# A two-stage kernel's hand-written order table replaced by another, searched with a later landing for DMA transposes

## The chip, the cores and the metric

The kernel runs on one core of a Trainium2 chip. The metric is device time in microseconds (us) of one execution; the value for a kernel is the median of several executions. The core has a matrix engine (TensorE, PE in the profile), a vector engine (VectorE, DVE), a scalar engine (ScalarE, ACT), GpSimd (POOL) and a sync engine (SyncE, SP) that here only issues DMAs. Each engine runs its own instructions in the order in which the program gives them; between engines, semaphores make one wait for another.

## The reference

Two stages, the first an attention with a decaying state, the second a mixing layer. Shapes: 4 batches, 8 heads, 768 tokens, head width 48 (8 x 48 = 384 channels).

```
for t in range(S):
    kt, vt, rt = (k[:, :, t], v[:, :, t], r[:, :, t])
    cur = np.einsum('bhd,bhe->bhde', u[None] * kt, vt)
    y[:, :, t] = np.einsum('bhd,bhde->bhe', rt, state + cur)
    state = w[None, :, :, None] * state + np.einsum('bhd,bhe->bhde', kt, vt)
...
theta = x @ w_theta
cos_t, sin_t = (np.cos(theta), np.sin(theta))
zr = x * cos_t
zi = x * sin_t
yr = np.einsum('ts,bsd->btd', w_tok_r, zr)
yi = np.einsum('ts,bsd->btd', w_tok_i, zi)
y = yr + yi
u = x + y
return (u + np.maximum(u @ w_ch, 0.0)).astype(np.float32)
```

Here x is the attention's y with the heads side by side, 4 x 768 x 384.

## The kernel before

**Tiling.** A batch's 768 tokens are 6 chunks of 128; two chunks make a pair. There are 12 pairs, numbered 0 to 11 over the batches. `attention` (one call for each pair) loads r, k and v, multiplies r and k by powers of the decay (`rscale`, line 567; `kscale`, 580 or 583), turns both so that the channels lie along the partitions (the "R flip" and "K flip": matmuls against the identity, line 530, then a copy out of PSUM), makes scores (631) and masks them (637), adds the product of r and k for the diagonal (PD, line 644 in batch 0 and 650 later; its sums at 659 go through `dg` to `yd`, 666), updates the state (outer 690, S 708 and 718), and makes the outputs (730, 735), to which line 742 adds yd: that is x in bf16. In batch 0 two tokens share a partition in the loads, and v is spread by matmuls (615).

**The turn of x and u.** x is turned to xT for theta (760). The first six pairs do this on TensorE, with a copy out of PSUM; from pair 6 on, `turn` (line 543) does it with a DMA transpose, issued from SP. theta is followed by sine and cosine on ACT (764, 767), and by zr on DVE (770) and zi on GpSimd (773). `mixing` (one call for each pair) sums 12 matmuls for each chunk over the batch's six zr and six zi chunks (791, two matmuls in a task), adds x (`un`, 800), turns the result to uT (on TensorE in pairs 0 to 3 and 11, by DMA transpose in pairs 4 to 10), multiplies with w_ch (`f`, the channel matmul, 817), finishes on DVE (`fin`, 821) and stores (825). The token weights are cast (291 or 289) and turned on TensorE (514) as they arrive, and copied from PSUM.

**Fillers.** 108 tasks of two matmuls on zeros (834) need no data. They stand in TensorE's order where the table puts them, and 32 of them after the last channel matmul.

**What sets the order.** `build` only describes the work: each call of `P.add` is a task with the engines that may run it, each with a pair of planned costs in ns (time on the engine, and time from then until the result can be used), and with what it reads and writes. 925 tasks come out. The order is written out in `ORDER`: one entry for each task, with its number, its engine (0 PE, 1 DVE, 2 ACT, 3 POOL, 4 SP) and, where it takes PSUM banks, their numbers. `follow` walks the table and emits the tasks; the planned costs are not used then. They were used by a search outside the program that made the table. In it, `lock=SHARED` marks tasks of DVE and POOL that the planner does not let overlap; when the program runs, nothing keeps them apart, unless data does.

The lines that set the transposes' planned cost and the order:

```
def turn(dst, src, prio, rd, wr, name):
    P.add({SP: (1600, 1500)}, lambda e: nc.sync.dma_start_transpose(out=dst, in_=src),
          rd=rd, wr=wr, prio=prio - 2e6, name=name)
...
for seq, e, *tiles in table:
    t = self.tasks[seq]
    assert all(d.seq in done for d in t.deps)
    done.add(seq)
    t.eng = ENGINES[e]
```

All loads, stores and transposes go through SP's one queue in table order; an entry that waits for a buffer or for data holds those behind it.

Of the kernel before, what the change touches and what calls it, by code (L numbers as in the profile page):

```python
# [27 lines left out]
    (0, 2), (4, 1), (13, 3), (2, 1), (3, 1), (16, 0, 7), (1, 2), (146, 4), (14, 3), (17, 0, 5),  # L28
    (7, 2), (145, 4), (8, 3), (10, 3), (9, 1), (32, 0, 2), (5, 1), (33, 0), (18, 2), (34, 0),
    (144, 4), (20, 2), (35, 0), (153, 3), (36, 0), (37, 0), (23, 2), (38, 0), (39, 0), (15, 3),  # L30
    (24, 2), (40, 0), (41, 0), (22, 2), (154, 0, 6, 0), (12, 3), (186, 4), (150, 1), (19, 2), (42,
    0), (21, 2), (11, 1), (43, 0), (6, 1), (44, 0), (25, 0, 3), (187, 4), (45, 0), (46, 0), (151,
    0, 5), (26, 1), (30, 1), (27, 2), (147, 1), (47, 0), (167, 0, 4), (152, 2), (48, 0), (49, 0),
    (50, 0), (168, 1), (51, 0), (188, 4), (52, 0), (53, 0), (28, 2), (54, 0), (155, 2), (55, 0),
    (189, 1), (31, 3), (56, 0), (148, 0, 3), (156, 2), (169, 0), (149, 2), (190, 0, 0), (229, 4),
    (192, 1), (57, 0), (58, 0), (59, 0), (191, 2), (60, 0), (61, 0), (157, 0, 1, 7), (170, 1),
    (62, 0), (63, 0), (163, 1), (64, 0), (228, 4), (193, 0, 6), (158, 1), (65, 0), (66, 0), (67,
    0), (195, 2), (68, 0), (69, 0), (164, 0, 5), (159, 1), (70, 0), (71, 0), (160, 0, 3, 4), (165,
    2), (194, 2), (230, 4), (166, 3), (196, 0, 1, 0), (161, 1), (72, 0), (73, 0), (209, 0, 7),
    (198, 2), (162, 1), (197, 2), (171, 0, 6), (140, 4), (234, 1), (74, 0), (210, 2), (75, 0),  # L40
    (76, 0), (202, 0, 3, 1), (29, 2), (199, 0, 0, 4), (172, 1), (231, 3), (173, 0, 5), (280, 4),
    (201, 1), (77, 0), (211, 0), (203, 1), (235, 0, 6), (272, 4), (237, 2), (78, 0), (79, 0),
    (174, 1), (80, 0), (81, 0), (82, 0), (83, 0), (212, 1), (84, 0), (236, 2), (232, 0, 4), (142,
    4), (205, 1), (85, 0), (86, 0), (87, 0), (251, 0, 7), (268, 4), (233, 2), (204, 1), (281, 3),
    (175, 0, 6), (200, 1), (88, 0), (141, 2), (206, 0, 1), (276, 4), (89, 0), (90, 0), (247, 1),
    (91, 0), (238, 0, 3, 0), (207, 2), (252, 2), (176, 1), (208, 3), (241, 0, 5, 4), (292, 4),
    (248, 0, 1), (240, 2), (243, 1), (213, 0, 7), (143, 2), (92, 0), (215, 0, 6), (242, 1), (249,
    2), (273, 2), (244, 0, 0, 4), (269, 3), (214, 1), (93, 0), (288, 4), (181, 0, 5), (239, 2),
    (216, 1), (270, 0, 1), (277, 2), (250, 3), (246, 1), (94, 0), (294, 4), (177, 0, 3), (271, 1),
    (182, 2), (217, 0, 4), (183, 2), (245, 1), (253, 0, 7), (293, 4), (218, 2), (297, 3), (95, 0),  # L50
    (96, 0), (97, 0), (254, 1), (278, 0, 6), (255, 0, 0), (178, 2), (184, 1), (282, 0, 4), (179,
    2), (284, 4), (256, 1), (223, 0, 5), (289, 2), (283, 1), (185, 3), (257, 0, 0), (296, 4),
    (180, 1), (219, 0, 7), (224, 2), (258, 2), (279, 1), (298, 0, 4), (98, 0), (274, 0, 3), (220,
    2), (333, 4), (300, 3), (99, 0), (221, 2), (100, 0), (290, 0, 0), (275, 1), (225, 2), (448, 0,
    6), (291, 1), (295, 4), (263, 0, 1), (299, 2), (222, 1), (449, 0), (285, 3), (441, 0, 0),
    (226, 1), (264, 2), (361, 4), (301, 0, 3), (265, 2), (227, 3), (259, 0, 4), (302, 1), (101,
    0), (442, 0), (260, 2), (266, 1), (443, 0), (363, 4), (261, 2), (450, 0), (310, 1), (267, 3),
    (286, 0, 1), (303, 2), (262, 1), (451, 0), (349, 4), (102, 0), (444, 0), (287, 1), (304, 0, 7,
    3), (307, 0, 4, 5), (314, 0, 1), (337, 4), (366, 3), (308, 1), (445, 0), (315, 2), (452, 0),
    (305, 1), (453, 0), (362, 4), (446, 0), (454, 1), (462, 0, 7), (311, 0, 4), (334, 3), (306,  # L60
    1), (463, 0), (357, 4), (312, 2), (350, 2), (464, 0), (447, 1), (313, 3), (465, 0), (466, 0),
    (402, 4), (316, 0), (335, 0, 4), (317, 1), (467, 0), (336, 2), (338, 3), (351, 0, 6), (468,
    1), (455, 0, 0), (352, 2), (318, 0, 3), (309, 1), (359, 4), (369, 3), (339, 0, 1), (367, 0,
    4), (319, 1), (345, 4), (340, 2), (320, 0, 7), (456, 1), (469, 0, 6), (368, 2), (321, 1),
    (470, 0), (341, 4), (370, 0, 0), (407, 3), (358, 2), (471, 0), (371, 1), (322, 0, 1), (364,
    4), (360, 2), (472, 0), (379, 1), (473, 0), (323, 2), (376, 0, 3, 7), (365, 4), (373, 0, 4,
    5), (346, 2), (377, 1), (474, 0), (324, 0, 0), (378, 1), (342, 2), (403, 4), (457, 0, 1),
    (475, 1), (328, 0, 7), (374, 1), (476, 0, 3), (404, 4), (329, 2), (380, 0, 6), (459, 0, 4),
    (477, 1), (381, 2), (325, 2), (375, 1), (343, 0, 6), (326, 2), (372, 3), (353, 4), (480, 0,
    3), (458, 1), (330, 2), (478, 0, 5), (327, 1), (382, 3), (344, 2), (347, 0, 1), (504, 4),  # L70
    (460, 1), (383, 0, 0), (348, 2), (479, 1), (408, 0, 6), (387, 0, 4), (481, 1), (384, 2), (410,
    3), (483, 0, 1), (331, 1), (405, 4), (484, 0), (409, 2), (388, 1), (389, 0, 5), (385, 0),
    (485, 0), (390, 1), (354, 2), (406, 4), (486, 0), (332, 3), (386, 1), (487, 0), (411, 0, 5),
    (505, 4), (355, 0, 3), (412, 1), (391, 0, 7), (509, 3), (356, 2), (488, 0), (420, 1), (506,
    4), (490, 0, 4), (392, 2), (414, 0, 6, 0), (417, 0, 5, 3), (415, 1), (491, 0), (544, 4), (413,
    3), (492, 0), (489, 1), (493, 0), (419, 1), (421, 0, 7), (494, 0), (495, 0), (422, 1), (416,
    1), (461, 4), (423, 3), (424, 0, 6), (510, 0, 1), (418, 1), (425, 2), (426, 0, 0), (507, 4),
    (496, 1), (511, 2), (629, 0, 3), (512, 3), (427, 1), (428, 0, 7), (622, 0, 5), (546, 4), (429,
    1), (103, 0), (397, 0, 0), (430, 0, 7), (398, 2), (497, 0, 1), (549, 3), (545, 4), (399, 2),
    (393, 0, 6), (431, 2), (513, 0, 4), (400, 1), (508, 4), (623, 0), (394, 2), (514, 1), (436, 0,  # L80
    7), (395, 2), (401, 3), (630, 0), (498, 1), (437, 2), (432, 0, 0), (547, 4), (396, 1), (438,
    2), (550, 0, 1), (522, 1), (433, 2), (499, 0, 6), (434, 2), (548, 4), (439, 1), (440, 3),
    (501, 0, 4), (551, 2), (500, 1), (631, 0), (435, 1), (632, 0), (684, 4), (515, 2), (516, 0, 7,
    6), (502, 1), (552, 3), (519, 0, 1, 0), (518, 1), (633, 0), (586, 4), (624, 0), (517, 1),
    (625, 0), (626, 0), (520, 1), (523, 0, 4), (555, 3), (585, 4), (526, 0, 6), (634, 0), (521,
    1), (524, 2), (527, 2), (627, 0), (525, 3), (635, 1), (553, 0, 1), (588, 4), (528, 0), (643,
    0, 0), (554, 2), (529, 1), (644, 0), (645, 0), (628, 1), (584, 4), (530, 0, 6), (562, 1),
    (566, 0, 7), (636, 0, 3), (567, 1), (650, 0, 5), (592, 3), (637, 2), (532, 0, 1), (531, 1),
    (587, 4), (646, 0), (533, 1), (568, 0), (563, 0, 3), (651, 0), (569, 1), (482, 4), (647, 0),
    (564, 1), (652, 0), (556, 0, 6, 7), (683, 4), (559, 0, 3, 4), (589, 3), (653, 0), (561, 1),  # L90
    (654, 0), (640, 0, 1), (558, 1), (595, 2), (655, 0), (534, 4), (557, 1), (593, 0, 7), (565,
    3), (648, 0), (641, 1), (670, 0, 4), (656, 1), (590, 0, 6), (685, 4), (560, 1), (671, 0),
    (591, 2), (570, 0, 5), (649, 1), (688, 3), (572, 0, 1), (571, 1), (723, 4), (606, 0, 3), (594,
    2), (573, 1), (663, 0, 0), (638, 0, 6), (607, 2), (602, 1), (664, 0), (665, 0), (574, 4),
    (639, 1), (599, 0, 1, 5), (596, 0, 3, 7), (691, 3), (601, 1), (672, 0), (603, 0, 6), (666, 0),
    (686, 4), (604, 1), (600, 1), (667, 0), (535, 0, 5), (598, 1), (605, 3), (539, 0, 6), (687,
    4), (536, 2), (597, 1), (673, 0), (540, 2), (668, 0), (537, 2), (575, 0, 3), (657, 4), (543,
    3), (669, 1), (541, 2), (608, 0, 1), (538, 1), (576, 2), (692, 0, 0), (542, 1), (577, 2),
    (610, 0, 5), (609, 1), (693, 2), (689, 0, 7), (503, 4), (611, 1), (674, 0), (694, 3), (675,
# [157 lines left out]
def build(ctx, tc, nc, r, k, v, w, u, moe_w_theta, moe_w_tok_r, moe_w_tok_i, moe_w_ch, out):  # L257
# [12 lines left out]
    P = Plan(SLOTS)  # L270
# [615 lines left out]
```

## Time and profile before

| | |
|---|---|
| median of 5 executions | 140.0 us (139.24 to 140.33) |
| the profiled execution | 139.24 us |
| its span in the profile | 137.5 us |
| granted TensorE clock in the span | 1.00 |
| PE instructions (matmuls) | 1670 |
| of them fillers (line 834) | 216 |
| DMA transposes | 13 (6 to xT, 7 to uT) |

A row of a group or timeline gives start and duration in us, the engine, the line of the program, the operation, what it writes and reads, and in brackets how long the engine had been idle and what released it. The second part of the page cuts the span into 40 slices of 3.4 us, with the busy share of each engine in tenths. A row of waits gives the waiting engine, line and tile, what it waited for, the total in us, the number of waits, and the longest. Matmuls overlap: a matmul's duration is longer than the time until the next one starts.

### The profile page before, as it was taken

The page shows a single profiled execution, that of the slowest core. Times are in us where ns is not written, and L with a number is a line of the kernel's source. Part 1 is how long each engine was busy: PE and PEld are TensorE (multiplying, and loading weights), DVE is VectorE, ACT ScalarE, POOL GpSimd, SP SyncE. Part 2 cuts the span into 40 slices and gives each one's busy share as a digit, 9 for nine tenths or more (in the row PEclk, how much of TensorE's full clock was granted, in tenths as well). Part 3 has the DMA queues.
Part 4 walks back from the last instruction along what each step waited for, and adds up shares of the span by engine and source line. Part 5 has one row for each costly group of instructions (what it writes and reads, how often), then busy time and mean ns, then how long its engine had stood idle before and what let it go on. Part 6 is the DMA issues. An engine that isn't in the chain of part 4 may idle for free.

```text
span 137.5 us, 4123 instructions
## 1 busy us (share of the span) xinstructions
PE 133.3 (97%) x1670; PEld 96.4 (70%) x1670; DVE 107.7 (78%) x208; ACT 77.2 (56%) x142; POOL 85.6 (62%) x77
## 2 busy tenths in 40 slices
PE   6999979999999999999999999999999998999995
PEld 3688767887668688686676766767667674556684
DVE  1399899997878898868986989888997997254750
ACT  3868878998649897469553347935016343310010
POOL 7613742999999369599999828779493066040000
DMA  3999999889999799999993739699794977304761
GB/s 96 272 261 261 311 395 321 168 238 255 318 323 241 174 266 199 270 182 180 192 311 76 174 64 179 162 184 258 171 204 109 227 176 119 114 0 87 227 218 44
DMA packets 72445, 27.60 MB, mean 201 GB/s; under 512 B 67049, under 2 KB 70890, under 8 KB 72426
## 3 DMA queue, kind: packets, MB, share of 16 engines
q1 hardware_dynamic: 72400, 27.34, 84.8%
q8 instruction: 13, 0.21, 0.7%
q14 instruction: 6, 0.05, 0.1%
q10 hardware_dynamic: 26, 0.00, 0.0%
HBM read 20.06 MB, written 4.72 MB: 180 GB/s over the span
## 4 chain that ended last, share of the span: by engine, by line
PE 89%; DMA 6%; DVE 2%; issue 0%; ACT 0%; DVEq 0%; ACTq 0%
PE bank L791 30%; PE bank L530 11%; PE bank L834 10%; PE bank L760 8%; PE bank L817 8%; PE bank L631 4%; PE bank L690 4%; DMA xT<-x 3%; PE bank L735 3%; DMA uT<-un 3%; PE bank L514 3%; PE bank L730 2%; PE bank L659 2%; DVE mAT L637 1%; PE bank L419 1%; PE bank L615 1%
## 5 line engine op out<-in xcount | busy, mean ns | idle before, releaser
L791 PE MATMUL bank<-zi,WiT 128*128 128x384 bf16 x144 | 33.7, 326 | 0.0
L637 DVE TENSOR_TENSOR mAT<-bank,mask 128x512 bf16<-128x512 f32 x48 | 30.9, 681 | 3.4 <-PE bank L631 3.1
L791 PE MATMUL bank<-zr,WrT 128*128 128x384 bf16 x144 | 33.2, 326 | 0.0
L666 POOL TENSOR_TENSOR yd<-dg,vb 128x768 bf16<-128x768 f32 x12 | 18.1, 1506 | 21.3 <-ACT vb L289 6.6
L773 POOL TENSOR_TENSOR zi<-x,sin 128x768 bf16<-128x768 bf16 x12 | 19.6, 1640 | 5.5 <-ACT sin L764 5.2
L764 ACT ACTIVATE sin<-bank 128x384 bf16<-128x384 f32 x24 | 11.9, 496 | 14.7 <-PE bank L760 11.7
L567 POOL TENSOR_TENSOR Rw<-ld,wpow 128x768 bf16<-128x768 f32 x10 | 18.2, 1820 | 0.0
L834 PE MATMUL bank<-zeros 128*128 128x128 bf16 x216 | 18.2, 231 | 0.0
L791 PEld LDWEIGHTS <-WiT 128*128 128x128 bf16 x144 | 12.8, 98 | 6.9
L791 PEld LDWEIGHTS <-WrT 128*128 128x128 bf16 x144 | 12.7, 97 | 6.9
L770 DVE TENSOR_TENSOR zr<-bank,x 128x384 bf16<-128x384 f32 x24 | 13.0, 550 | 5.0 <-ACT bank L767 5.0
L583 POOL TENSOR_TENSOR Kw<-ld,wpinv 128x768 bf16<-128x768 f32 x9 | 16.4, 1819 | 0.6 <-DMA ld<-in_k_dram 0.6
L834 PEld LDWEIGHTS <-zeros 128*128 128x128 bf16 x216 | 14.2, 103 | 3.0 <-issue 2.0
L821 DVE SCALAR_TENSOR_TENSOR fin<-bank,un 128x384 f32<-128x384 f32 x24 | 12.9, 551 | 4.0 <-PE bank L817 3.9
L760 PE MATMUL bank<-Wth,xT 128*128 128x384 bf16 x72 | 15.3, 326 | 0.2 <-DMA xT<-x 0.2
L289 ACT ACTIVATE RT<-bank 128x1024 bf16<-128x1024 bf16 x12 | 12.3, 1031 | 5.4 <-PE bank L530 5.3
L817 PE MATMUL bank<-Wch,uT 128*128 128x384 bf16 x72 | 14.8, 326 | 0.4 <-DMA uT<-un 0.4
L800 DVE TENSOR_TENSOR un<-bank,x 128x384 bf16<-128x384 f32 x24 | 13.0, 550 | 2.2 <-PE bank L791 1.7
L742 DVE TENSOR_TENSOR x<-bank,yd 128x384 bf16<-128x384 f32 x24 | 12.9, 551 | 0.9 <-PE bank L735 0.6
L767 ACT ACTIVATE bank<-bank,pi 128x384 f32<-128x384 f32 x24 | 13.2, 566 | 0.0
L289 ACT ACTIVATE Sb<-bank 64x192 bf16<-64x192 f32 x20 | 6.5, 324 | 7.8 <-PE bank L690 7.6
L817 PEld LDWEIGHTS <-uT 128*128 128x128 bf16 x72 | 6.6, 98 | 4.5 <-DMA uT<-un 0.8
(96 smaller groups left out, 216.4 us busy)
## 6 DMA issues: line engine op xcount, KB each, us to landing
ld<-in_r_dram SPq DMA_DIRECT2D x12, 384.0 KB, 5.5
out_dram<-fin SPq DMA_DIRECT2D x11, 384.0 KB, 2.8
ld<-in_k_dram SPq DMA_DIRECT2D x18, 192.0 KB, 5.2
ld<-in_v_dram SPq DMA_DIRECT2D x18, 192.0 KB, 4.2
ld<-in_moe_w_tok_i_dram SPq DMA_DIRECT2D x6, 384.0 KB, 6.7
ld<-in_moe_w_tok_r_dram SPq DMA_DIRECT2D x6, 384.0 KB, 5.5
ld<-in_v_dram SPq DMA_DIRECT2D x3, 384.0 KB, 5.6
ld<-in_k_dram SPq DMA_DIRECT2D x3, 384.0 KB, 6.2
```

The lines of the kernel that those rows point to most:

```text
L289: nc.scalar.activation(dst, src, Act.Copy)
L530: nc.tensor.matmul(bank16(tok)[:, i * C:(i + 1) * C], s, ident, is_transpose=True, start=(i == 0), stop=(i == n - 1))
L567: P.add(mul(g, 2.15), lambda e: eng_of[e].tensor_mul(Rw[:, :, :, :D].transpose([0, 2, 1, 3]), Ls[ir].rearrange("p (h n d) -> p h n d", h=H ...
L583: eng_of[e].tensor_mul(Kw[:, :, :, :D].rearrange("p a h d -> p (a h) d"), Ls[ik].rearrange("p (a d) -> p a d", d=D), wpinv.rearrange("p a ...
L637: P.add({DVE: dve_op(4 * C)}, lambda e, tk=tk[hi], c=c, hi=hi: nc.vector.tensor_mul(mAT[:, c, hi], bank(tk).rearrange("p (h t) -> p h t", ...
L666: P.add({POOL: pool_op(2 * HD, 1.7)}, lambda e: eng_of[e].tensor_mul(yd.rearrange("p a (h d) -> p (a h) d", h=H), wide(dg, D), vb.rearrang ...
L760: nc.tensor.matmul(bank(th)[:, :HD], xT[:, ND * c + dk, :], Wth[:, dk, :], start=(dk == 0), stop=(dk == ND - 1))
L767: P.add({ACT: act_op(HD, True, True)}, lambda e, th=th: nc.scalar.activation(bank(th)[:, :HD], bank(th)[:, :HD], Act.Sin, bias=pi2), use=[th],
L773: P.add({POOL: pool_op(2 * HD, 1.9)}, lambda e: eng_of[e].tensor_mul(zi[:, 2 * pr:2 * pr + 2], x[:, 2 * pr:2 * pr + 2], sn), rd=xk + [("si ...
L791: nc.tensor.matmul(bank(tm)[:, :HD], WT[:, so, to * C:(to + 1) * C], z[:, so], start=(so == 0 and part == 0), stop=(part == 2 * NP - 1 and ...
L817: nc.tensor.matmul(bank(tf)[:, :HD], uT[:, ND * t + dk, :], Wch[:, dk, :], start=(dk == 0), stop=(dk == ND - 1))
L834: nc.tensor.matmul(bank("warm")[:, :C], zeros, zeros, start=True, stop=True, skip_group_check=True)
```

## The change

The table `ORDER` is another one, and the second planned cost of a DMA transpose is 2000 ns instead of 1500. No task is added or removed, no instruction is changed, and each task has the same dependencies. As the table alone makes the order, the program differs only in the order on each engine, in which engine runs some tasks, and in which PSUM bank some results take.

```diff
 ORDER = [
-    (0, 2), (4, 1), (13, 3), (2, 1), (3, 1), (16, 0, 7), (1, 2), (146, 4), (14, 3), (17, 0, 5),
-    (7, 2), (145, 4), (8, 3), (10, 3), (9, 1), (32, 0, 2), (5, 1), (33, 0), (18, 2), (34, 0),
-    (144, 4), (20, 2), (35, 0), (153, 3), (36, 0), (37, 0), (23, 2), (38, 0), (39, 0), (15, 3),
+    (0, 2), (4, 1), (12, 3), (2, 1), (3, 1), (16, 0, 6), (6, 1), (1, 2), (144, 4), (10, 3), (17,
+    0, 3), (8, 3), (7, 2), (14, 3), (9, 1), (11, 1), (145, 4), (5, 1), (32, 0, 2), (13, 3), (33,
+    0), (18, 2), (34, 0), (146, 4), (23, 2), (35, 0), (36, 0), (37, 0), (24, 2), (38, 0), (39, 0),
...
     def turn(dst, src, prio, rd, wr, name):
-        P.add({SP: (1600, 1500)}, lambda e: nc.sync.dma_start_transpose(out=dst, in_=src),
+        P.add({SP: (1600, 2000)}, lambda e: nc.sync.dma_start_transpose(out=dst, in_=src),
               rd=rd, wr=wr, prio=prio - 2e6, name=name)
```

What the two tables differ in, read off them:

- **Engines.** 34 tasks change engine; DVE goes from 200 to 203 tasks, ACT from 134 to 129, POOL from 61 to 63. In the first part: the k scales of pairs 1 and 2 from DVE to POOL; the r scale of pair 2 from POOL to DVE; the copies of xT of pairs 1 and 2 and the dg of pair 2 from ACT to DVE; the first Wr copy from DVE to ACT. Later ones are casts of token weights, copies from PSUM, v casts and a few state and dg copies.
- **The opening on PE.** Before: 10 fillers, the v spread of pair 0, 3 fillers, the small transpose of w and u (line 433), 2 fillers, the K flip of pair 0, a filler, an outer product, 9 fillers, the R flip. After: 17 fillers, the small transpose, the K flip, the R flip, 8 fillers, the outer product, 5 fillers, the v spread.
- **Fillers.** Ahead of the last channel matmul task 76 stand before and 77 after; the other 32 and 31 stand behind it.
- **DVE's opening.** The Sb memsets (line 369) and the ident cast (386) stand ahead of the first k scale instead of behind it.
- **Loads.** The first three are v, k, r of pair 0 before, and r, k, v after. A part of w_theta and the first row of w_tok_r come ahead of r and v of pair 2; other rows of the token weights change places.
- **Transposes.** Their order among themselves is the same, but the PE work between what they need and who reads them is another; loads and stores between them move. The x of pair 7 stands behind two loads and a store after, behind two loads before.

## The prediction

> **What bounds the kernel.** I read the page's first two parts, then the chain, then PE's own waits, then the timeline at each place where PE waits.
>
> ```profile
> PE 133.3 (97%) x1670; PEld 96.4 (70%) x1670; DVE 107.7 (78%) x208; ACT 77.2 (56%) x142; POOL 85.6 (62%) x77
> ...
> PE   6999979999999999999999999999999998999995
> ...
> DVE  1399899997878898868986989888997997254750
> ...
> PE 89%; DMA 6%; DVE 2%; issue 0%; ACT 0%; DVEq 0%; ACTq 0%
> ```
>
> TensorE is full from the second slice on. All of its work stays, so only what lies between its instructions can change. Its waits after the opening are three small ones:
>
> ```profile
> PE bank L530 <- DVE x L742: 0.8, 1, 0.8
> PE bank L817 <- DMA uT<-un: 0.4, 1, 0.4
> PE bank L760 <- DMA xT<-x: 0.2, 1, 0.2
> ```
>
> Matmul ends are modelled, so I measure each wait as start to next start, less the median of that kind (mix 0.325, theta and f 0.487, a filler 0.112 once warm, RT or KT flip 0.447). That gives 0.89, 0.60 and 0.38 us. Between 28 us and the last channel matmul at 132.25, the two DMA waits, 0.98 in all, are the only stalls over 0.1; the others are about 0.1 each, before a scores task. The places in the timeline (start, duration, engine, line, idle before and its releaser):
>
> ```profile
> 16.14 2.55 DVE L580 TENSOR_TENSOR Kw<-ld,wpinvj 128x768 bf16<-128x768 f32 x1
> 18.61 0.55 DVE L742 TENSOR_TENSOR x<-bank,yd 128x384 bf16<-128x384 f32 x1
> ...
> 16.05 1.82 POOL L567 TENSOR_TENSOR Rw<-ld,wpow 128x768 bf16<-128x768 f32 x1
> ...
> 19.20 0.61 PE L530 MATMUL bank<-ident,Kw 128*128 128x128 bf16 x8 [0.82 <-DVE x L742]
> ...
> 79.89 1.24 SPq L543 DMA_TRANSPOSE xT<-x  x1
> ...
> 84.53 0.66 PE L760 MATMUL bank<-Wth,xT 128*128 128x384 bf16 x3 [0.21 <-DMA xT<-x]
> ...
> 112.60 1.22 SPq L543 DMA_TRANSPOSE uT<-un  x1
> ...
> 116.78 0.66 PE L817 MATMUL bank<-Wch,uT 128*128 128x384 bf16 x3 [0.44 <-DMA uT<-un]
> ```
>
> Two transposes were read 4.6 and 4.2 us after issue. The trace gives a landing for nine of the thirteen: five at 2.7 or 2.8 us, four at 4.1 to 4.6. The old table allowed 1.6 + 1.5 = 3.1, the new one 3.6, so it still covers only the quick ones by itself.
>
> How far can the table be trusted elsewhere? I took each of the 395 tasks on DVE, ACT and POOL and compared its start with that of the PE task that follows it in the table. 367 start earlier, and only two start over 0.5 us later: x of pair 0 and the mask behind it, at 18.6 and 19.1, both queued behind the 2.55 us scale. So the planned costs hold on this chip except in two places: DMA transposes, and VectorE and GpSimd scales that meet.
>
> **The change part by part.**
>
> PE content. The same 434 PE tasks run. Ahead of the last channel task stand 77 fillers instead of 76: +0.11. The opening: before, 15 fillers and the V spread (0.755 cold, 0.38 warm) run before the first K flip at 8.09; after, 17 fillers at about 0.225 from 3.83 and the 0.20 wu transpose, so the flip can start at 7.86. Net: -0.23 at the start, two fillers fewer later but one more in all (-0.11), V now warm but later (+0.38): +0.04. Its inputs are there: the k scale on DVE runs 6.18 to 7.14 and waits for k, the second load in both tables. The Sb memsets (0.84) and the ident cast (0.22) moved ahead of it fall into its 1.90 us wait. r, now first, lets the r scale follow at 7.05 to 8.0, against a flip due at 8.31. v, now third, is first used at about 9.6.
>
> DMA transposes. For each I summed the PE time that the table puts between the last PE task its input needs and the first matmul that reads it. Old to new, us: xT of pairs 6 to 11: 10.00 to 9.48, 5.24 to 6.22, 4.72 to 5.41, 7.25 to 5.66, 4.64 to 7.11, 4.06 to 4.39. uT of pairs 4 to 10: 10.68 to 11.16, 7.85 to 12.10, 8.19 to 8.60, 6.91 to 10.89, 4.49 to 5.96, 4.23 to 4.50, 4.87 to 4.99. Needed: from the PE end to the issue (0.83 and 0.74 at the two stalls, DVE's add and its queue) plus the landing: 3.6 with a quick one, 5.2 to 5.5 with a slow one. Both that stalled, xT 7 and uT 8, are now past that: the 0.98 goes. What is late next: xT 11 and uT 9 and 10, at 4.39, 4.50 and 4.99, short by 0.86, 0.75 and 0.26 if each lands slowly (5.25), by nothing if quickly. Their nearest rows are their own before: issued at 114.44, 123.89 and 125.5 and used 3.8, 3.3 and 4.0 us later with no stall, so all three landed quickly. Ends: from -0.98 to +0.9; I take -0.8, nearest to their own rows with a little left for chance. Queue: SP issues in order, and each transpose keeps its neighbours but for moved loads and outs. Pair 7's xT now stands behind an out (0.57) and two loads issued ahead of it; its slack of 0.7 over the slow case covers that out.
>
> Early engines. The k scales of pairs 1 and 2 go from DVE (1.58 and 2.55) to POOL (1.82 each by the other nine L583), and pair 2's r scale from POOL to DVE (0.96 by the two on DVE). Two xT evictions (0.54) and one dg (0.17) come to DVE, one Wr eviction (0.54) leaves. DVE from 9 to 28 us, where it is busy 18.65 of 19: -4.13 + 0.96 + 1.08 + 0.17 - 0.54 = -2.5. That work is on the path: DVE set the 0.89 stall.
>
> Against this speaks the Trainium skill, "SBUF — State Buffer", section "Who interferes with whom": a VectorE instruction with two SBUF inputs and a GpSimd instruction that reads SBUF share a port, and the later to issue is blocked until the other ends. The rows agree: POOL's scale ends at 17.87, and DVE's ends 0.82 later, about its own 0.96 alone; likewise the 1.58 one behind POOL's wS (9.94 to 11.50). By the rule two POOL scales can each block one PD product (pairs 0 to 2 read RT and KT, both SBUF) for up to 1.82, so 3.6 back on DVE: -2.5 becomes +1.2. By the unblocked PD row (0.67 to 0.68 at 12.71, 21.20, 23.00) nothing comes back. Which starts first is not in the old trace. For PE: from -0.9 (stall gone) to +1.2. I take -0.3: one block of about 1.8 leaves DVE 0.7 lighter, a third of the way.
>
> Loads. theta's small half and the first Wr row are loaded before pair 2's r and v. An estimate from the load bytes in table order at the GB/s row's early 262, set by the load that POOL waited for until 19.89: the r of pair 3 comes at about 25.2 and its scale is due at 25.4, so that cover is down to 0.2. I cost it at nothing; each us that it lands later is a stall of the same size at pair 3's R flip. Other casts, evictions and v copies that change engine between 30 and 110 us sit beside a full PE at old slacks of 0.3 to 2; nothing.
>
> Tail: from the last channel task to the end 5.2 us of 137.5 both times, with the same outs.
>
> **Sum.** +0.04 - 0.8 - 0.3 = -1.06. The profiled execution took 139.24 (span 137.5 and 1.7 around it): 138.2. It was the quickest of five, 0.8 under the median, and nothing shown says why; the same step from 140.0 gives **138.9**.
>
> **Rivals.**
> A, given back: the DMA waits go, but another wait takes their place (one more port block, or xT 11 landing slowly); or the landings vary so that another table place stalled in other executions. For: four slow landings among nine. Against: every distance under 7 us grew; of the longer ones only xT 9's comes near the slow case (5.66). Time: +0.04 - 0.8 + 0.7 = about 139.9.
> B, slower: both POOL scales take the port ahead of a PD product. For: DVE has no slack from 15 to 28 us, POOL starts early when its input lands (POOL's scale started at 16.05 without waiting for DVE's). Against: POOL's scales now come when DVE is lighter. Price +1.2, and with the late pair 3 load +0.6 on it, less 0.8 and with the 0.04: 141.0. It decides once a PD starts after its POOL scale by less than 0.7 us in both places.
> That the distances don't matter, because quick landings are the rule: then only the early part acts; inside A.
>
> **Chances.** The forecast 0.56 (its own range 138.1 to 139.4), A 0.18, B 0.26. 0.5% (0.7 us) is about what can be told from no change. Faster: 0.46 from the forecast and 0.04 from A, 0.50. Same: 0.08, 0.12 and 0.02, 0.22. Slower: 0.02, 0.02 and 0.24, 0.28. Range: the best of both bounds is -1.9, 138.1, less 0.5 for the spread of such medians, 137.6; upward past B to 141.2, short of both worst ends together (142.1).
>
> **What would show it.** PE's waits: no DMA line but perhaps xT 11; L530 behind x gone or under 0.4. DVE's PD rows (L644) at 0.68 confirm the early part, at 1.5 to 2.5 rival B. PE's first K flip at 7.9. Last channel task's end near 131.2. Wrong if a PE wait over 1 us stands before 32 us, or on a transpose of pair 11 or 9.

## The result, and the profile after

| | before | after |
|---|---|---|
| median | 140.0 us (138.25 to 140.97) | 138.23 us (137.41 to 139.43) |
| ratio of after to before, 95% interval | | 0.9911 (0.9886 to 0.9936) |
| profiled execution | 139.24 us | 137.15 us |
| its span | 137.5 us | 135.4 us |
| start of the last channel matmul task (817) | 131.60 us | 129.74 us |

The ratio is worked out from runs taken in turn on the same chips and leaves out executions over 1.5% longer than the quickest of their kernel (two of the 25 of after, and two of the six of e10 below). Times 140.0 it gives 138.75, a gain of 1.25 us (0.9 to 1.6). The medians of all runs differ by more, 1.77. The profiled execution of after was quicker than the other 24, which begin at 137.41, so the 2.09 between the two profiles flatter the change; one thing that differs between executions of the new table is shown behind e9.

First the page of after: its span, the busy time of each engine, two rows of the 40 slices (tenths of busy time, 3.4 us each) and the chain of waits.

```profile
span 135.4 us, 4125 instructions
...
PE 132.3 (98%) x1670; PEld 96.5 (71%) x1670; DVE 107.6 (79%) x211; ACT 75.0 (55%) x135; POOL 88.1 (65%) x79
...
PE   6999999999999999999999999999999999999995
...
DVE  5299698998978997998698988978897896174750
...
PE 94%; DMA 4%; issue 0%; DVE 0%
```

DVE's share of the chain falls from 2% to 0%, PE's rises from 89% to 94%, and a DMA still holds 4%. In the slices PE is at 9 from the second on; the 7 and the 8 of before are gone. PE's own waits in after (engine, line, what it waited for, total us, times, longest):

```profile
PE bank L416 <- DVE zeros L364: 1.1, 1, 1.1
PE bank L817 <- DMA uT<-un: 0.4, 1, 0.4
```

Of the three waits shown of before, the one behind x is gone and the one for xT is gone. A line for uT stands there with the same 0.4, but it is another task: before it was pair 8's, at 116.78; now it is pair 6's, at 105.16.

Adding up, by kind of PE task, the time from each start to the next start, up to the last channel task, says where the 1.86 us came from:

| kind of PE task | before to after, us | what it is |
|---|---|---|
| outer products (690) | -0.89 | the stall behind x is gone |
| v spread (615) | -0.33 | no longer at half clock |
| fillers (834) | -0.07 | two more at half clock ahead of the flip (+0.37), later fewer that take 0.2 (-0.44) |
| channel matmuls (817) | -0.50 | the wait for uT of pair 8 |
| mix (791) | -0.35 | the wait for xT of pair 7 |
| K flips (530) | +0.61 | ahead of pair 6's f: the new wait for uT |
| scores (631), R flips, diagonal, theta | -0.20, -0.10, -0.07, +0.10 | waits of about 0.1 each |

The rest is -0.06. From that last start to the end of the span, another 0.22 is saved (5.92 to 5.71).

**The early part.** VectorE and GpSimd of after, between 10 and 26 us (start, duration, engine, line, operation, idle before and its releaser):

```profile
10.32 0.76 DVE L644 TENSOR_TENSOR PD<-RT,KT 128x1024 bf16<-128x1024 bf16 x1
...
17.78 0.68 DVE L644 TENSOR_TENSOR PD<-RT,KT 128x1024 bf16<-128x1024 bf16 x1
...
23.21 1.00 DVE L644 TENSOR_TENSOR PD<-RT,KT 128x1024 bf16<-128x1024 bf16 x1
```

```profile
10.63 2.12 POOL L580 TENSOR_TENSOR Kw<-ld,wpinvj 128x768 bf16<-128x768 f32 x1
...
14.76 1.82 POOL L580 TENSOR_TENSOR Kw<-ld,wpinvj 128x768 bf16<-128x768 f32 x1
...
24.08 1.81 POOL L567 TENSOR_TENSOR Rw<-ld,wpow 128x768 bf16<-128x768 f32 x1 [0.40 <-DMA ld<-in_r_dram]
```

The two k scales now run on GpSimd, and no PD product is held for the length of one. The first scale meets the first PD at 10.63 and is itself the one that is longer (2.12 for 1.82), as PD started 0.31 ahead of it; the second runs from 14.76 to 16.58, when no PD is near. The 1.00 at 23.21 stands beside casts on GpSimd. The last row is the r of pair 3, 0.40 late; PE has no wait there.

**The new wait.** What SP issued around pair 6's uT in after, with the two operations on VectorE that make its inputs ready, and the matmul that reads it:

```profile
95.85 1.02 DVE L800 TENSOR_TENSOR un<-bank,x 128x384 bf16<-128x384 f32 x2 [0.36 <-PE bank L791]
96.94 1.02 DVE L742 TENSOR_TENSOR x<-bank,yd 128x384 bf16<-128x384 f32 x2
...
98.02 1.22 SPq L543 DMA_TRANSPOSE xT<-x  x1
99.28 0.58 SPq L825 DMA_DIRECT2D out_dram<-fin  x1
99.96 1.26 SPq L543 DMA_TRANSPOSE uT<-un  x1
...
105.16 0.66 PE L817 MATMUL bank<-Wch,uT 128*128 128x384 bf16 x3 [0.42 <-DMA uT<-un]
```

un is done at 95.85 + 1.02 = 96.87, but its transpose is issued at 99.96. In SP's queue it stands behind pair 9's xT, which waits for an x that is done at 97.96, and behind a store that the new table moved ahead of it. So 3.1 us of the distance to its reader go by before the transpose starts, and 5.2 more until the read, longer than the slow landings of before (4.1 to 4.6). Both have a part in the wait: the last section shows what the slow landings have in common.

### The profile page after: what moved, and what is told of

Same layout as the page of the kernel before. It is cut to its first block, busy times and chain, and to the rows that moved or that the text cites. A ratio compares the mean times of both kernels' runs of the same rounds, so it can differ in the third digit from the quotient of the medians.

```text
span 135.4 us, 4125 instructions
## 1 busy us (share of the span) xinstructions
PE 132.3 (98%) x1670; PEld 96.5 (71%) x1670; DVE 107.6 (79%) x211; ACT 75.0 (55%) x135; POOL 88.1 (65%) x79
## 3 DMA queue, kind: packets, MB, share of 16 engines
HBM read 20.06 MB, written 4.72 MB: 183 GB/s over the span
## 4 chain that ended last, share of the span: by engine, by line
PE 94%; DMA 4%; issue 0%; DVE 0%
PE bank L791 34%; PE bank L834 11%; PE bank L530 11%; PE bank L817 9%; PE bank L760 8%; PE bank L631 5%; DMA uT<-un 4%; PE bank L690 3%; PE bank L735 3%; PE bank L514 3%; PE bank L730 2%; PE bank L659 2%; PE bank L419 1%; PE bank L416 1%; PE bank L698 1%; PE bank L615 1%
## 5 line engine op out<-in xcount | busy, mean ns | idle before, releaser
L834 PEld LDWEIGHTS <-zeros 128*128 128x128 bf16 x216 | 14.7, 106 | 2.9 <-issue 1.7
L567 POOL TENSOR_TENSOR Rw<-ld,wpow 128x768 bf16<-128x768 f32 x9 | 16.3, 1817 | 0.4 <-DMA ld<-in_r_dram 0.4
L817 PE MATMUL bank<-Wch,uT 128*128 128x384 bf16 x72 | 15.1, 326 | 0.4 <-DMA uT<-un 0.4
L760 PE MATMUL bank<-Wth,xT 128*128 128x384 bf16 x72 | 14.5, 326 | 0.0
L289 ACT ACTIVATE KT<-bank 128x1024 bf16<-128x1024 bf16 x9 | 9.2, 1027 | 5.5 <-PE bank L530 5.5
L289 ACT ACTIVATE uT<-bank 128x768 bf16<-128x768 bf16 (+1 forms) x5 | 3.4, 684 | 11.9 <-PE bank L530 11.9
```

Of the source, the lines that this page charges most:

```text
L289: nc.scalar.activation(dst, src, Act.Copy)
L567: P.add(mul(g, 2.15), lambda e: eng_of[e].tensor_mul(Rw[:, :, :, :D].transpose([0, 2, 1, 3]), Ls[ir].rearrange("p (h n d) -> p h n d", h=H ...
L760: nc.tensor.matmul(bank(th)[:, :HD], xT[:, ND * c + dk, :], Wth[:, dk, :], start=(dk == 0), stop=(dk == ND - 1))
L817: nc.tensor.matmul(bank(tf)[:, :HD], uT[:, ND * t + dk, :], Wch[:, dk, :], start=(dk == 0), stop=(dk == ND - 1))
L834: nc.tensor.matmul(bank("warm")[:, :C], zeros, zeros, start=True, stop=True, skip_group_check=True)
```

## The experiments

Twelve kernels, each compared with the kernel before. They are named by label. In those called h1, e6, e7, e9, e10, e12 and e13 the line numbers are one higher (L818 is L817 of before). A diff of the table is given by its entries. Where fillers are left out, no part of the result is: nothing reads them.

### Which part of the table brings it: h1_early_new, h2_late_new, e3_kscale2_on_pool

```diff
 # h1: the first 330 entries of the new table, then the rest in the old order
 # h2: the first 330 entries of the old table, then the rest in the new order
 # e3: the old table with one entry changed: the k scale of pair 2 on GpSimd
-(234, 1)
+(234, 3)
```

> The first 330 entries of the new table (to about 32 us), then the old order for the rest. My theory: the early part brings most of the gain (port stall of 0.89 and 0.4 of the opening in the profiles), so about 1.2 us under before, ratio 0.991 to 0.993, no PE wait over 0.2 us before 32 us, and the DMA waits of the old late part still there by chance. Rival (the late reads of the transposes bring it): ratio 0.998 to 1.000.

> The first 330 entries of the old table, then the new order for the rest. My theory: the port stall near 18 us stays (PE waits 0.8 to 0.9 for x), and the late part saves 0.4 (profiles: 0.98 of DMA waits before, 0.58 after), ratio about 0.997. Rival (late reads bring it): ratio 0.991 to 0.993.

> The old table with one entry's engine changed: the k scale of pair 2 on GpSimd instead of VectorE. Theory of the port: GpSimd does both scales one after the other, no VectorE task lasts 2.5 us, x of pair 0 starts near 16.6 instead of 18.6, the PE wait of 0.82 goes; time 0.7 to 0.9 under before, ratio 0.994. Rival (the stall only moves, since the K flip of pair 2 needs that scale, and the r scale of pair 2 ends 1.8 later): a PE wait at the K or R flip of pair 2, ratio 0.998 to 1.002.

**h1**: 139.26 us, 0.997 (0.9938 to 1.0002), less of a gain than the 0.991 to 0.993 expected. Its PE waits:

```profile
PE bank L417 <- DVE zeros L365: 1.1, 1, 1.1
PE bank L818 <- DMA uT<-un: 0.8, 1, 0.8
PE bank L515 <- ACT dg L290: 0.6, 1, 0.6
PE bank L761 <- DMA xT<-x: 0.3, 1, 0.3
```

The stall behind x is gone (outer products -0.85 from before, v spread -0.34), and the two late waits of the old order are there. But at the seam of the two tables, at 48.27, a wait stands (0.71, measured start to start) that neither table has alone. Without it the ratio would be near 0.992, an estimate from this one profile; the run itself doesn't show that the early part brings most of the gain.

**h2**: 139.65 us, 0.9988 (0.9952 to 1.0024). Its PE waits:

```profile
PE bank L416 <- DVE zeros L364: 1.1, 1, 1.1
PE bank L530 <- DVE x L742: 0.8, 1, 0.8
PE bank L817 <- DMA uT<-un: 0.5, 1, 0.5
PE bank L530 <- DVE Rw L567: 0.2, 1, 0.2
```

The stall behind x stays; the waits for xT 7 and uT 8 are gone, and the new one, uT of pair 6, is there (0.63 start to start). So the late half of the new table gives back much of what it saves. The two halves' intervals overlap and don't add up to the whole by themselves: the seam of h1 stands in the way.

**e3**: 139.33 us, 0.9949 (0.9922 to 0.9975): 0.7 us for one entry. GpSimd and VectorE around the place of the old stall, in e3:

```profile
16.67 1.82 POOL L580 TENSOR_TENSOR Kw<-ld,wpinvj 128x768 bf16<-128x768 f32 x1
17.22 0.56 DVE L742 TENSOR_TENSOR x<-bank,yd 128x384 bf16<-128x384 f32 x1 [0.38 <-PE bank L735]
18.45 1.83 POOL L567 TENSOR_TENSOR Rw<-ld,wpow 128x768 bf16<-128x768 f32 x1
```

With both scales on GpSimd they follow each other there, x is made at 17.22 instead of 18.61, and VectorE even waits for PE ahead of it. The outer products come down by 0.88, as in after.

### The same part, undone in the new table: e9_scales_back

```diff
-(192, 3)  (234, 3)  (231, 1)
+(192, 1)  (234, 1)  (231, 3)
```

> The new table with the three scales on the engines of the old one: k scales of pairs 1 and 2 on VectorE, r scale of pair 2 on GpSimd. Theory of the port: VectorE meets GpSimd again, a scale of 1.5 to 2.6 us on VectorE and PE waits of 0.8 to 1.8 before 30 us; 0.9 to 1.5 above the new kernel, ratio to before 0.998 to 1.002. Rival (the new order, not the engine, brought the early gain): ratio 0.990 to 0.993.

139.05 us, 0.9946 (0.9923 to 0.9968): some 0.35% or 0.5 us above after, between the two theories; the intervals just overlap. The row that rival B feared, PD held by a GpSimd scale, appears here, in the version that has fewer scales there:

```profile
17.71 1.82 POOL L568 TENSOR_TENSOR Rw<-ld,wpow 128x768 bf16<-128x768 f32 x1 [0.52 <-PE bank L616]
18.55 1.51 DVE L645 TENSOR_TENSOR PD<-RT,KT 128x1024 bf16<-128x1024 bf16 x1
...
20.12 0.35 PE L660 MATMUL bank<-uw,PD 128*128 128x2 bf16 x8 [0.28 <-DVE PD L645]
```

The scale ends at 19.53, PD at 20.06, 0.53 later and 0.83 longer than the 0.68 of an undisturbed one. PE pays 0.28 for it. So a scale on GpSimd can block PD.

It can with the new table's engines too. In e6, a kernel of the next section, every entry up to 90 us is that of after, but the first meeting goes the other way round:

```profile
10.54 1.81 POOL L581 TENSOR_TENSOR Kw<-ld,wpinvj 128x768 bf16<-128x768 f32 x1
10.78 2.12 DVE L645 TENSOR_TENSOR PD<-RT,KT 128x1024 bf16<-128x1024 bf16 x1 [0.36 <-ACT RT L290]
...
PE bank L660 <- DVE mAT L638: 0.7, 1, 0.7
```

Here the scale starts first, PD takes 2.12 instead of 0.76, and PE waits for the mask behind it; from start to next start that costs 0.86, and 1.96 in e12. That is nearly what the removed stall cost. Seven profiles have this scale on GpSimd in the new opening (start of pair 0's R flip on PE, start of PD, start of the scale, and how long the two took):

| profile | R flip | PD starts | scale starts | PD, us | scale, us |
|---|---|---|---|---|---|
| after | 8.14 | 10.32 | 10.63 | 0.76 | 2.12 |
| h1 | 8.00 | 10.35 | 10.69 | 0.77 | 2.12 |
| e7 | 8.13 | 10.31 | 10.55 | 0.77 | 2.19 |
| e10 | 8.18 | 10.35 | 10.52 | 0.73 | 2.24 |
| e13 | 8.12 | 10.33 | 10.61 | 0.71 | 2.10 |
| e6 | 8.57 | 10.78 | 10.54 | 2.12 | 1.81 |
| e12 | 8.53 | 10.74 | 10.64 | 2.25 | 1.81 |

PD needs RT, a copy of what the R flip makes, and in e6 and e12 it waits for it. There the R flip came 0.4 later, because TensorE still ran the K flip ahead of it at half speed (last section). So the table leaves it open which of the two is first, and when the half speed ends decides it in these seven. The 24 times of after lie in two groups, 13 from 137.41 to 138.25 and 11 from 138.69 to 139.43, while those of e9, which hasn't this meeting, lie in one, 138.56 to 139.53. That would fit a block in about half of the executions of after, but it isn't shown: the one profile of after is without it, and the 22 times of h1, which has the meeting, show no such gap.

### The late waits: e5_later_reads, e5c_f8_later_own_bank, e6_ut6_first

If the distance between a transpose and its reader is what counts, moving the readers later in the old table should remove its two DMA waits.

```diff
 # e5, old table: theta of pair 7 (first chunk, with its sine and cosine) moved behind a mix task,
 # f of pair 8 (856, 857) moved behind the mix task 870
 # e5c, old table: only the second of these, with a PSUM bank of its own
-(856, 0, 1)
+(856, 0, 4)
```

> The old table with only two reads of DMA transposes later: theta of pair 7's first chunk by 2.3 us of PE work, f of pair 8's first chunk by 0.98. Theory that these two waits cost 0.98 in each execution: 0.98 under before, ratio 0.993, no DMA line in PE's waits. Rival (which landing is slow changes from execution to execution, so the wait is paid now and then, and at other reads too): 0.2 to 0.5 under before, ratio 0.997 to 0.999.

> The old table with f of pair 8's first chunk three mixes (0.98 us) later and in a PSUM bank of its own, so that theta of pair 11 need not wait for its fin as in the run before. Theory of the late landing: the wait at that f (0.60, 0.97 and 0.84 us in three profiles of this late order) goes, nothing takes its place, ratio 0.994 to 0.996. Rival (the time is given back at the next read, xT of pair 11 or the mixes of batch 3): ratio 0.998 to 1.001.

**e5**: 141.16 us, 1.0103 (1.0051 to 1.0155), slower. PE no longer waits for a transpose, and other waits have come. One of them, VectorE and PE of e5:

```profile
88.70 0.56 DVE L770 TENSOR_TENSOR zr<-bank,x 128x384 bf16<-128x384 f32 x1 [1.85 <-ACT bank L767]
...
89.31 0.65 PE L817 MATMUL bank<-Wch,uT 128*128 128x384 bf16 x3 [0.87 <-DVE zr L770]
```

The theta that was moved later makes its zr late; zr stands in VectorE's queue and blocks it for 1.85 us, with what f of PE needs behind it. A second wait (0.6, theta for fin) came because the moved f keeps its PSUM bank 1, which pair 11's theta wants next. Both are the price of moving single entries by hand, so e5 doesn't test the distances.

**e5c**: 139.08 us, 0.994 (0.9894 to 0.9987). With f of pair 8 alone moved, and its own bank, its wait is gone from the trace and nothing behind it took its place; xT of pair 7 still costs its 0.3, and the stall behind x its 0.8. A wait of 0.5 for an r scale near 11 us is new and far ahead of what was moved. So more distance does remove uT 8's wait, as far as one profile and this interval show it.

In the new table the queue is the suspect for pair 6's uT. In e6 it is issued ahead of pair 9's xT and of the store:

```diff
-(713, 4) xT of pair 9 ... (662, 4) out ... (815, 4) uT of pair 6
+(815, 4) uT of pair 6 ... (713, 4) xT of pair 9 ... (662, 4) out
```

> The new table with one entry moved: the transpose of u of pair 6 ahead of that of x of pair 9 (and of the store between them) in SP's queue; u has been ready since 96.9, x until 98.0, and u's transpose was issued at 99.96. Theory of the queue: it is issued near 97, the wait of f of pair 6 (0.58) goes, theta of pair 9 doesn't wait (issue 0.2 later, 4.4 to its read): 0.5 under the new kernel, ratio to before about 0.987 to 0.988. Rival (its landing was late by itself, or theta of pair 9 waits instead): ratio 0.991 as for the new kernel.

137.6 us, 0.9851 (0.9798 to 0.9903). SP of e6:

```profile
98.22 1.22 SPq L544 DMA_TRANSPOSE uT<-un  x1
...
99.53 1.25 SPq L544 DMA_TRANSPOSE xT<-x  x1
```

The time from the start of pair 11's K flip to the f of pair 6 falls from 1.03 to 0.45, and xT of pair 9 is still in time. That is a saving of 0.58 in the trace. The ratios of e6 and of after overlap, so in the time it isn't told apart; the profiled execution of e6 took 138.12 against 137.15, with the block of PD described above. That the place in the queue was needed for the wait is shown by the trace.

### The fillers: e7, e10, e12, e13, b_half_fillers

PE is 98% busy in after, and every wait that is removed moves work forward. But 55 fillers stand between real work from 8.6 to 30.4 us. If that work is ready earlier than the table's planned costs say, fillers delay it.

```diff
-                for _ in range(2):
+                for _ in range(2 if COND else 0):
                     nc.tensor.matmul(bank("warm")[:, :C], zeros, zeros, start=True, stop=True,
 # e7,  new table:              COND = not 17 <= i < 72               (55 fillers empty)
 # e10, e6's table:             COND = not (17 <= i < 72 and i % 2)   (28)
 # e12, e6's table:             COND = not (17 <= i < 72 and i % 3)   (37)
 # e13, e10 with the last two ahead of the K flip empty as well       (30)
 # b_half_fillers, old table:   COND = not (17 <= i < 71 and i % 2)   (27)
```

> The new table without the matmuls of the 55 fillers between the first K flip and about 30 us (55 x 0.112 = 6.2 us of TensorE); the fillers at the opening and behind the last channel task stay. Theory that VectorE, ACT and the loads set the pace there: TensorE waits where the fillers stood, the first mix comes at most 1 us earlier, ratio 0.985 to 0.991. Rival 1 (the fillers hold real work back): 2 to 5 us less, ratio 0.96 to 0.98. Rival 2 (the granted clock falls where TensorE idles): slower, over 1.00, with rows of double length.

> e6's order with every second one of those 55 fillers without its matmuls (28 x 0.112 = 3.1 us). If real work stands ready behind fillers, up to 3 us under e6; if other engines set the pace, as e6 within 0.3 us, TensorE idle in the places of the fillers, clock full.

> The old table with every second of its 54 fillers between the first K flip and about 35 us without its matmuls (27 x 0.112 = 3.0 us). If fillers are in the way in both tables: ratio 0.975 to 0.985, and the new table's lead over the old one stays about 0.9% between the two thinned kernels. Rival (in the old table the port stall and VectorE set the pace): ratio 0.993 to 1.000, TensorE idle instead; then the new table's gain was that it made room for thinning.

> e6's order with two of three of the 55 early fillers thinned (36 of them, 4.0 us). The half-thinned one left TensorE waits of about 1 us there and the full thinning about 5: I expect the gain to be used up near half, ratio 0.966 to 0.970 as for the half, with waits near 3 us; below 0.965 if fillers still held work back.

> As the half-thinned e6 order, and two of the 17 opening fillers ahead of the small transpose thinned too (0.44 at half speed). The first K scale ended at 7.03 and the flip began at 7.69, so the flip can begin near 7.25: 0.4 under the half-thinned kernel, ratio 0.965, if the clock is full by then; no gain or a loss if the clock, not the fillers, sets the opening.

| kernel | table | fillers emptied | median, us | ratio to before |
|---|---|---|---|---|
| b_half_fillers | old | 27 | 136.93 | 0.9793 (0.975 to 0.9836) |
| e7_no_early_fillers | new | 55 | 136.08 | 0.972 (0.9675 to 0.9765) |
| e12_third_fillers | new, uT 6 first | 37 | 136.4 | 0.975 (0.9696 to 0.9804) |
| e10_ut6_half_fillers | new, uT 6 first | 28 | **135.31** | 0.9676 (0.9625 to 0.9726) |
| e13_half_and_opening | new, uT 6 first | 30 | 135.39 | 0.9693 (0.9636 to 0.9751) |

Three of the same stretch, 8 to 30 us, in after, e10 and e7 (the stretch; its length, then the busy us and instructions of PE, PE's weight loads, DVE, ACT and POOL; granted clock, DMA share, GB/s):

```profile
8.00:30.00 22.00, 22.00 (x406) 18.56 (x404) 20.36 (x36) 18.73 (x34) 18.07 (x16) 1.00 1.08 281
```

```profile
8.00:30.00 22.00, 20.92 (x363) 16.56 (x360) 21.19 (x37) 19.37 (x36) 18.83 (x16) 1.00 1.11 293
```

```profile
8.00:30.00 22.00, 18.88 (x316) 14.28 (x314) 21.36 (x37) 19.75 (x37) 19.03 (x16) 1.00 1.08 286
```

In after 108 of the 406 matmuls are fillers, in e10 54 of 363, in e7 none. Real matmuls in the same 22 us: 298, 309, 316. PE's busy share falls from 100% to 95% to 86%, and it gets more done; DVE's rises from 93% to 96% to 97%, so that DVE is then the fullest engine of this stretch. The clock is 1.00 in all three profiles.

It isn't in every execution. Two of the six of e7 and two of the six of e10 have a granted clock of 0.987 over their span. Those of e10 took 137.75 and 137.97, against 135.05 to 135.44 for its other four; those of e7 took 136.09 and 137.44, against 134.98 to 136.18. No other execution with a recorded clock is under 1.00: not the 18 of b, e12 and e13, nor the more than 200 of kernels with all their fillers. So emptying fillers seems to risk some clock, as the second rival of e7 said, though here the gain outweighs it. What set the clock back in these four stays open, as there is no trace of them. With all six counted, the means are 136.1 for e7 and e10, 136.3 for e12, 135.7 for e13 and 136.9 for b.

That e7 isn't the fastest fits with PE's waits in it, for VectorE, ScalarE and pair 6's uT: those of 0.2 and up add to 3.4 us without the opening's 1.1. In e10 the same sum is 0.9, in e12 2.7, with one of 1.8 behind a mask: that one is PD held by the k scale. So the profile of e12, which missed its expected 0.966 to 0.970, has a worse opening than that of e10 and doesn't tell what two thirds are worth. The intervals of the last four rows overlap, so the order among them isn't sure. That thinning helps is, with either table, and every execution of the version with half the fillers and pair 6's uT first was below the median of either kernel. The old table with half its fillers still has the stall behind x, and a larger one:

```profile
PE bank L530 <- DVE x L742: 1.3, 1, 1.3
```

e13 brought the first K flip from 7.72 in e10 to 7.29 and gained nothing: there the flip ran at half speed (the R flip follows 0.83 later, not 0.45). The last section says more of this.

## Why the prediction was right, and where its terms were off

The forecast was 138.9 and faster; the measured ratio times 140.0 is 138.75. The sum was -1.06 us, and the ratio gives -1.25. Its terms, against the profile of after:

| term | predicted | measured |
|---|---|---|
| opening and fillers | +0.04 | -0.40 |
| DMA transposes | -0.8 | -0.98 + 0.58 = -0.40 |
| early engines | -0.3 | -0.89 |
| loads | 0 | 0 on PE |
| all other waits up to the last channel task | 0 | -0.17 |
| tail | 0 | -0.22 |

That the sum came so near is in part luck. Only the loads and the v spread came out as priced, the other misses have both signs, and the profile's terms add up to -2.08, the ratio to -1.25.

**Opening.** The K flip came at 7.69 (7.86 was predicted). The v spread saved its 0.33 against 0.38 predicted. The miss is the fillers, which I had priced at +0.34 together (+0.23 more ahead of the flip at the cold rate, +0.11 for the one that is added) and which came to -0.07. A little of that, 0.09, lies ahead of the flip: the 17 took 3.74 us and not 17 x 0.225. The larger part, 0.33, lies behind it. There every filler was priced at 0.112, but one that stands right ahead of a scores, v-spread, diagonal or outer task can take 0.16 to 0.23 from its start to the next. The old table has eight such fillers behind the flip and the new one four. The other profiles with the same opening and all fillers have nearly the same ones, so this comes from the table and isn't chance. The end of the half speed plays no part in it: in both profiles all fillers ahead of the flip ran at half speed.

**DMA transposes.** That xT 7 and uT 8 would be in time was right, and so, for uT 8, was the cause: in e5c its wait goes with more distance alone. Of the pairs next in line none stalls, as expected: xT 11 landed in 3.15 us and uT 10 in 2.74 (the trace has no landing for uT 9). The failed step is "each transpose keeps its neighbours but for moved loads and outs". I measured the distance from the PE task that un needs to the reader, 8.60 for pair 6's uT, and took the queue to cost it nothing. But a transpose ahead of it waits for its own x, and an out was moved in between: 3.1 of the 8.60 were spent there, and the read was 0.58 late. e6, which changes only this, is free of the wait. A slow landing had been allowed for as well, of 4.6 at most; this one took some 5.2.

**Early engines.** The stall of 0.89 is gone in after, and it is gone in e3 with one entry: the mechanism held. The -0.3, "one block of about 1.8", looks too careful beside the -0.89 of after's profile, but the block is real. In e6, with the same early entries, PE saved 0.90 and paid 0.86. So the -0.3 lies between the two cases, and it is luck that the profile of after shows the better one. The question left open, which starts first, isn't settled by the table at all. Rival B needed the block in both places. It came in one at most: the second scale and the second PD lie apart in every profile of the new opening with all fillers and new engines (0.68 in after, h1 and e6). The rule of the Trainium skill that I weighed against the gain ("SBUF — State Buffer", "Who interferes with whom") does price a meeting rightly: 0.83 for PD in e9. e9 gives what the engine change is worth in the new table, 0.5 us (0.35%), and e3 in the old one, 0.7.

**Loads.** The r of pair 3 came sooner than estimated, at 24.08 and not 25.2, but its scale was due sooner as well and waited 0.40 on GpSimd. PE has no wait there, as priced.

**Rival A**, given back, happened in part: another wait took the place of the two. It took 0.58 where A had 0.7, but at pair 6, which I had called safe, and not at pair 11, and the early part paid for it.

**"TensorE is full, so only what lies between its instructions can change"** was right for this change, which keeps all fillers, and wrong as a reading of the kernel: e10 takes 28 of them out and is 1.7% under e6, which has the same order (135.31 against 137.6). The page counts a filler as busy.

"Quick" and "slow" landings were taken as chance. They go with the place: the last section shows that the waits for xT 7, uT 8 and, in after, uT 6 each meet a load of instructions, and why b_half_fillers, which has the old late order, has none of them.

The share of each term in the ratio can't be given better than some 0.3 us, which is what the intervals leave.

## What to carry to other kernels

A busy engine isn't a bound engine where some of its work is filler: count the useful instructions in a stretch, then take the fillers out by halves and see which engine is late next, and look at the granted clock of every execution, not of one profile. A transfer's slack is counted from the moment its queue can issue it, so for each one look at what the entries ahead of it wait for, not only at its own input and reader. Where two engines meet within 0.3 us of each other, take one profile as one draw, and look at others. Before an order is searched anew, change the single entry at which the worst stall stands; here one engine number alone gave 0.7 us, and the whole new table 1.25.

## What the runs showed of the hardware

**The opening's half speed ends at a different time in each execution.** All fourteen profiles have much the same PE activity up to 7 us, and PE is busy from 1.05 on. The last two matmuls of 128 columns that start 107 and not 56 ns apart do so at: before 7.90, after 7.18, h1 6.84, h2 8.99, e3 9.01, e5 7.40, e5c 6.95, e6 8.47, e7 7.17, e9 6.67, e10 7.17, e12 9.38, e13 8.44, b_half_fillers 8.97. The old opening has both 6.95 and 9.01, the new one 6.67 and 9.38. The granted-clock column says 1.00 all along. Six traces hold the moment itself as well, and it lies up to 0.8 later, where no such pair ran in between: after 7.53, e5 7.90, e13 8.56, e6 8.64, e3 9.38, h2 9.81. The first K flip in after and in e3, PE's timeline:

```profile
7.69 0.62 PE L530 MATMUL bank<-ident,Kw 128*128 128x128 bf16 x8
8.14 0.61 PE L530 MATMUL bank<-ident,Rw 128*128 128x128 bf16 x8
```

```profile
8.16 1.06 PE L530 MATMUL bank<-ident,Kw 128*128 128x128 bf16 x8
9.01 0.42 PE L834 MATMUL bank<-zeros 128*128 128x128 bf16 x2
```

Eight matmuls to the next row: 0.45 in after, 0.85 in e3. A spread of 2.7 us in this moment is up to 1.35 us of work, an estimate, and so may be a good part of the 2 to 3 us between the quickest and slowest run of one kernel. Single profiles of two tables can differ by as much, and by what follows from it, as the order of PD and scale above. The Trainium skill ("TensorE: Matmul & The Clock Gate", Part 1) states that the change varies by 500 ns either way from run to run; the fourteen profiles here show more.

**What a meeting of VectorE and GpSimd costs.** The scales and PD read two operands from SBUF. Where one of them starts on one engine while an operation of the other engine that reads SBUF is under way, it takes longer by what that one still needs, less 0.13 to 0.15 us. Some of the rows of the traces:

| the later one, its start, its time alone | the earlier one | left of it | longer by |
|---|---|---|---|
| before: k scale, VectorE, 16.14, 0.96 | r scale, GpSimd | 1.73 | 1.59 |
| before: k scale, VectorE, 10.73, 0.96 | wS, GpSimd | 0.77 | 0.62 |
| e6: PD, VectorE, 10.78, 0.68 | k scale, GpSimd | 1.57 | 1.44 |
| e12: PD, VectorE, 10.74, 0.68 | k scale, GpSimd | 1.71 | 1.57 |
| e9: PD, VectorE, 18.55, 0.68 | r scale, GpSimd | 0.98 | 0.83 |
| after: PD, VectorE, 23.21, 0.68 | cast, GpSimd | 0.46 | 0.32 |
| after: k scale, GpSimd, 10.63, 1.82 | PD, VectorE | 0.45 | 0.30 |
| e9: r scale, GpSimd, 24.52, 1.82 | PD, VectorE | 0.58 | 0.44 |

Beside a memset on GpSimd, which reads nothing, a k scale on VectorE kept its 0.96 (e3, with 0.28 left). So the cost of a meeting follows from the two starts and the length of the earlier operation.

**Slow landings meet a load of instructions.** The page of both kernels lists, beside the data, the packets that bring the program's own instructions:

```profile
q8 instruction: 13, 0.21, 0.7%
```

They are 16 KB each, take 0.9 to 1.5 us, and come about every 10 us for most of the span. The packets of the traces give their times:

| transpose | issued | instruction packet | landed |
|---|---|---|---|
| before, xT of pair 7 | 79.89 | 82.24 to 83.28 | 84.48 |
| before, uT of pair 8 | 112.60 | 114.48 to 115.50 | 116.74 |
| h1, uT of pair 8 | 111.87 | 114.33 to 115.26 | 116.37 |
| e3, uT of pair 8 | 112.13 | 114.50 to 115.46 | 116.50 |
| b_half_fillers, uT of pair 8 | 111.80 | 110.07 to 111.00 | 114.57 |
| after, uT of pair 6 | 99.96 | 102.97 to 103.91 | read at 105.16 |

All eleven waits of PE for a transpose in these traces (over 0.2 us) have a packet that starts 1.9 to 3.1 us after the issue, and ten of them end 1.0 to 1.3 us after it does. Of the 114 landings that the traces give, 69 took 2.70 to 2.85 us, and only three of these have a packet under way between 1 us after the issue and the landing. 45 took longer, and 34 of these have one; the other eleven aren't explained. b, with 54 matmuls fewer, has its packet earlier in the work, ahead of uT 8, which lands in 2.77 us, and on uT 7, which takes 5.50. In after the place in the queue kept uT 6 back until it met its packet; in e6 it is issued at 98.22, and the packet comes only at 104.22. No run moved a packet alone, so that it holds the transpose back is read from these times and not tested.
